# Cached attention with a token mixer on one core: the order of the last loads and of the last two pairs' steps

## Chip, cores and metric

The kernel runs on one NeuronCore of a Trainium2 chip. The metric is the device time of one execution in microseconds; lower is better.

## The reference

Two blocks work on the same normalised input and are added to it:

```python
xn = layernorm(x)                              # x: (8, 1, 512)
# A: grouped-query attention over a cache, one new token per sequence
q = (xn @ wq) in 32 heads of 128               # wq: (512, 4096)
k, v = caches of 8 heads x 8192 keys x 128     # per sequence, f32; 4 query heads share one
o = softmax(q k^T / sqrt(128)) v
A = o @ wo                                     # wo: (4096, 512)
# B: token mixer, an MLP over the token axis (one token), 1792 wide
B = gelu(layernorm(xn) * w1 + b1) . w2 + b2
out = x + A + B
```

All is f32. The caches of keys and values are 2 x 8 x 8 x 8192 x 128 x 4 bytes, some 537 of the 554 MB that the kernel loads; every byte of them is used once.

## The kernel before

The work is 64 pairs of a sequence and a key-value head (`N_IT`, numbered 0 to 63; `i = h * 8 + b`). Each pair has one load of keys and one of values, 4 MB each: a tile of 128 partitions x 64 rows x 128 numbers. The tiles lie in a ring of five buffers (`raw`, `RING = 5`), so a load takes the buffer of the load five places before it and can be issued when that one's readers are done.

**The loads.** `order` (lines 53 to 58) lists all loads with a sort key; `load_next` (L68) issues the next one on SyncE's DMA queue, each time some step frees a buffer: at the end of `qk(i)`, the scores of a pair (which frees its keys), and at the end of `pv(i)`, its values matmuls (which frees its values). The sort keys `2 i` for keys and `2 i + 2.5` for values make keys and values alternate, except for the last: `min(i, N_IT - 1.9)` gives keys 63 the key 124.2, and so the order at the end is keys 62, keys 63, values 61, values 62, values 63. Most loads are one DMA. Keys 0 come in four pieces of 16 rows, values 63 in pieces of 32, 16, 8 and 8 rows. When the list is empty, the next call loads the output weights of the last two heads into a ring buffer, in eight DMAs of 256 KB, four for each head (L82 to L86). The output weights of the other heads are loaded in the loop by `load_wo`.

**The steps of a pair.** `turn` (L215) transposes a quarter of the keys in 32x32 blocks, in place, on VectorE (L218). `qk` (L222) makes the scores on TensorE (L228), all four quarters being needed. `sm_max` takes the maximum of each partition on VectorE (L238); `sm_bias` spreads these over the partitions on TensorE (L243) and makes the correction from them on VectorE (L246); `sm_exp` makes the exponentials on ScalarE (L252); `sm_place` permutes them on TensorE (L259) and transposes them on VectorE (L261). `pv` (L267) multiplies them with the values on TensorE (L272); it can be called for a part of its 16 blocks of four rows. `o_pick` keeps the right blocks, three VectorE instructions (L283 to L287), and `o_place` puts them in place on TensorE (L294); for the last pair `o_last` does both in another way (L299, L300, L303). At a head's end come `o_sums` (L311, L313), `o_scale` (L316) and `o_project`, the product with the output weights (L326) that is added to `yacc` (L328).

**The order.** The kernel's instructions are issued on each engine in the order in which they are written (`manual_schedule`). `slot(i)` (L380) is one pair of the loop, for pairs 0 to 61, and interleaves the steps of pair i with the turns of pair i + 1 and the values matmuls of pair i - 1; the mixer's steps (`mx_begin`, `mx_step`, `mx_end`) are spread over the slots. The end, lines 418 to 445, is an order of its own, written out by hand, for the scores and softmax of pairs 62 and 63, the values matmuls of 61, 62 and 63, and the last projection.

Of the kernel before, what the change touches and what calls it, by code (L numbers as in the profile page):

```python
# [14 lines left out]
B, D, HQ, HKV, SK, DH, F = 8, 512, 32, 8, 8192, 128, 1792  # L15
REP = HQ // HKV
P = 128
NT = SK // P
# [9 lines left out]
N_IT = B * HKV  # L28
# [5 lines left out]
def attn_mixer_kernel(ctx: ExitStack, tc: tile.TileContext, x, kc, vc, wq, wo, w1, b1, w2, b2, out):  # L34
# [12 lines left out]
    def misc():  # L47
        return ps_m.tile([P, 512], F32, name="misc")
# [3 lines left out]
    KR, VR = {}, {}  # L52
    order = []
    for i in range(N_IT):
        order.append((2 * min(i, N_IT - 1.9), kc, KR, i))
        order.append((2 * i + 2.5, vc, VR, i))
    order.sort(key=lambda o: o[0])
    order.reverse()
# [9 lines left out]
    def load_next():  # L68
        if order:
            _, src, to, i = order.pop()  # L70
            h, b = divmod(i, B)
            t = ring.tile([P, NT, DH], F32, name="raw")
            rows = src[b, h].rearrange("(p t) d -> p t d", p=P)
            at = 0
            for n in (NT // 4,) * 4 if to is KR and i == 0 else (NT // 2, NT // 4, NT // 8, NT // 8) if not order else (NT,):
                nc.sync.dma_start(t[:, at:at + n, :], rows[:, at:at + n, :])
                at += n
            to[i] = t
        elif HKV - 1 not in wos:
            t = ring.tile([P, NT, DH], F32, name="raw")  # L80
            t = t.rearrange("p (h r c) d -> p h r (c d)", h=4, r=REP)
            for h in (HKV - 2, HKV - 1):  # L82
                rows = wo[h * REP * DH:(h + 1) * REP * DH, :].rearrange("(r p) n -> p r n", p=P)
                wos[h] = t[:, h % 2]
                for r in range(REP):
                    nc.sync.dma_start(wos[h][:, r, :], rows[:, r, :])  # L86

    wos = {}
# [15 lines left out]
    for _ in range(RING - 2):  # L104
        load_next()
# [109 lines left out]
    def turn(i, a, w=NT // 4):  # L215
        if i < N_IT:
            t = KR[i][:, a:a + w, :].rearrange("p t d -> p (t d)")
            nc.vector.transpose(t, t)  # L218
# [3 lines left out]
    def qk(i):  # L222
        h, b = divmod(i, B)
        S[i] = ps_s.tile([P, 512], F32, name="s")
        kt = KR.pop(i).rearrange("p (u g) d -> p g u d", g=NG)
        for j in range(NB):
            for g in range(NG):
                nc.tensor.matmul(S[i][g * Q:(g + 1) * Q, :], W[h % 2][:, b, j, :], kt[:, g, :, j * Q:(j + 1) * Q],  # L228
                                 start=(j == 0), stop=(j == NB - 1))
        load_next()  # L230
# [5 lines left out]
    def sm_max(i):  # L236
        mr = work.tile([P, 1], F32, name="mr")
        nc.vector.tensor_reduce(mr, S[i], AX.X, ALU.max)  # L238
        st[i] = mr

    def sm_bias(i):
        m = misc()
        nc.tensor.matmul(m[:, :P], st[i].to_broadcast([P, P]), ident, start=True, stop=True)  # L243
        t = one.tile([P, P], F32, name="sq")
        nb = work.tile([P, 1], F32, name="nb")
        nc.vector.tensor_tensor_reduce(t, m[:, :P], hmask, -SCALE, 3.0e38, ALU.add, ALU.min, nb)  # L246
        st[i] = nb

    def sm_exp(i):
        h, b = divmod(i, B)  # L250
        p = t2k.tile([P, 512], F32, name="t2k")
        nc.scalar.activation(p, S.pop(i), AF.Exp, bias=st[i], scale=SCALE, accum_out=LR[h % 2][:, b:b + 1])  # L252
        st[i] = p
# [3 lines left out]
    def sm_place(i):  # L257
        m = misc()
        nc.tensor.matmul(m, perm, st.pop(i), start=True, stop=True)  # L259
        PT[i] = work.tile([P, 512], F32, name="pt")  # L260
        nc.vector.transpose(PT[i], m)  # L261
# [5 lines left out]
    def pv(i, u0=0, u1=NU):  # L267
        if u0 == 0:
            O[i] = ps_o.tile([P, 512], F32, name="o")
        for u in range(u0, u1):  # L270
            c = u % NB
            nc.tensor.matmul(O[i][c * Q:(c + 1) * Q, :], PT[i][:, u * Q:(u + 1) * Q],  # L272
                             VR[i][:, u * NG:(u + 1) * NG, :].rearrange("p t d -> p (t d)"),
                             start=(u < NB), stop=(u >= NU - NB))
        if u1 == NU:
            del VR[i], PT[i]
            load_next()
# [3 lines left out]
    def o_pick(i):  # L281
        om = t2k.tile([P, 512], F32, name="t2k")
        nc.vector.tensor_tensor(om.rearrange("p (g d) -> p g d", g=NG), O.pop(i).rearrange("p (g d) -> p g d", g=NG),  # L283
                                dm.unsqueeze(2).to_broadcast([P, NG, DH]), ALU.mult)
        ob = work.tile([P, 256], F32, name="ob")
        nc.vector.tensor_add(ob, om[:, :256], om[:, 256:])  # L286
        nc.vector.tensor_add(ob[:, :DH], ob[:, :DH], ob[:, DH:])  # L287
        OB[i] = ob

    def o_place(i):  # L290
        h, b = divmod(i, B)
        if b == 0:
            MH[h] = ps_h.tile([P, 512], F32, name="mh")
        nc.tensor.matmul(MH[h][:, b * REP:(b + 1) * REP], OB.pop(i)[:, :DH], sel, start=True, stop=True)  # L294
# [13 lines left out]
    def o_sums(h):  # L308
        m = misc()
        for r in range(REP):  # L310
            nc.tensor.matmul(m[:, r * B:(r + 1) * B], sel[:, r:r + 1].to_broadcast([P, P]), LR[h % 2], start=True, stop=True)  # L311
        RD[h] = work.tile([P, REP, B], F32, name="rd")
        nc.vector.reciprocal(RD[h], m[:, :REP * B].rearrange("p (r b) -> p r b", r=REP))  # L313
# [60 lines left out]
    quart = NT // 4  # L374
# [3 lines left out]
    LAST = N_IT - 1  # L378
# [39 lines left out]
    h = HKV - 1  # L418
    qk(LAST - 1)
    turn(LAST, 0)  # L420
    sm_max(LAST - 1)
    turn(LAST, quart)
    sm_bias(LAST - 1)
    sm_exp(LAST - 1)
    turn(LAST, 2 * quart)
    sm_place(LAST - 1)
    turn(LAST, 3 * quart)
    qk(LAST)
    sm_max(LAST)
    sm_bias(LAST)  # L430
    sm_exp(LAST)
    pv(LAST - 2)
    o_pick(LAST - 2)
    o_place(LAST - 2)
    sm_place(LAST)
    pv(LAST - 1)
    o_pick(LAST - 1)
    o_place(LAST - 1)
    o_sums(h)
    for u0, u1 in ((0, 8), (8, 12), (12, 14), (14, 16)):  # L440
        pv(LAST, u0, u1)
    o_last(LAST)
    o_scale(h)
# [29 lines left out]
```

## Time and profile before

| | us |
|---|---|
| median of 3 runs | 1305.3 (1303.94 to 1306.02) |
| the profiled execution | 1303.8 |
| its span, first to last instruction | 1301.9 |
| busy in the span: TensorE matmuls, VectorE, ScalarE, GpSimd | 791.1, 805.8, 289.4, 231.0 |
| DMA, mean over the span | 426 GB/s, 554.5 MB |

The profile is one execution. PE is TensorE, PEld its weight loads, DVE VectorE, ACT ScalarE, POOL GpSimd, SP SyncE, which issues the DMAs; a q behind the name is the engine's sequencer, which issues and waits. A line such as L228 is a line of the kernel. A row of the timeline has the start and the length in microseconds, the engine, the line and operation, the tile written and those read, their shapes, the count of instructions merged in the row, and in brackets the idle time before it and what ended that. A row of the DMA issues has the count, the size of each and the time from issue to landing. The list of waits has the waiting engine and line, whom it waited for, the total, the count and the longest. A float32 matmul stands as two instructions in the counts: 16 matmuls of `pv` are 32.

### The profile page before, as it was taken

The page shows a single profiled execution, that of the slowest core. Times are in us where ns is not written, and L with a number is a line of the kernel's source. Part 1 is how long each engine was busy: PE and PEld are TensorE (multiplying, and loading weights), DVE is VectorE, ACT ScalarE, POOL GpSimd, SP SyncE. Part 2 cuts the span into 40 slices and gives each one's busy share as a digit, 9 for nine tenths or more (in the row PEclk, how much of TensorE's full clock was granted, in tenths as well). Part 3 has the DMA queues.
Part 4 walks back from the last instruction along what each step waited for, and adds up shares of the span by engine and source line. Part 5 has one row for each costly group of instructions (what it writes and reads, how often), then busy time and mean ns, then how long its engine had stood idle before and what let it go on. Part 6 is the DMA issues. An engine that isn't in the chain of part 4 may idle for free.

```text
span 1301.9 us, 12448 instructions
## 1 busy us (share of the span) xinstructions
PE 791.1 (61%) x5178; PEld 260.6 (20%) x5178; DVE 805.8 (62%) x834; ACT 289.4 (22%) x365; POOL 231.0 (18%) x244
## 2 busy tenths in 40 slices
PE   3375657755566646656558556575465775576466
PEld 2121112111121112211113111121112211122112
DVE  2676575575665665665765756755666657656662
ACT  0032221221222321212202213023121223213210
POOL 1022211212112211212112112022120222113210
PEclk9688777777778678687687786777776777767778
DMA  9999999999999999999999999999999999999995
GB/s 403 434 434 428 429 434 431 434 432 431 431 432 435 430 434 433 431 430 430 434 431 433 433 432 428 434 433 431 430 432 433 432 435 432 435 432 430 429 432 216
DMA packets 24139, 554.50 MB, mean 426 GB/s; under 512 B 2540, under 2 KB 2572, under 8 KB 6932
## 3 DMA queue, kind: packets, MB, share of 16 engines
q1 hardware_dynamic: 23940, 553.67, 98.9%
q8 instruction: 41, 0.67, 0.2%
q14 instruction: 14, 0.11, 0.0%
q0 software_dynamic: 128, 0.02, 0.0%
q10 hardware_dynamic: 16, 0.02, 0.0%
HBM read 553.69 MB, written 0.02 MB: 425 GB/s over the span
## 4 chain that ended last, share of the span: by engine, by line
DMA 58%; PE 22%; DVE 13%; issue 4%; ACT 3%; SPq 0%; ACTq 0%; DVEq 0%
DMA raw<-in_A_k_cache_dram 56%; DVE raw L218 10%; PE s L228 10%; PE o L272 6%; PE misc L259 3%; ACT L252 2%; DMA raw<-in_A_wq_dram 2%; DVE mr L238 1%; ACT t2k L252 1%; PE s L188 1%; PE misc L336 1%; PE misc L326 1%; PE misc L311 0%; DVE t2k L283 0%; DVE sq L246 0%
## 5 line engine op out<-in xcount | busy, mean ns | idle before, releaser
L218 DVE STREAM_TRANSPOSE raw<-raw 128x2048 f32<-128x2048 f32 x256 | 582.1, 2294 | 347.8 <-DMA raw<-in_A_k_cache_dram 347.8
L228 PE MATMUL s<-raw,w 128*32 128x512 f32 x2048 | 324.3, 790 | 20.3 <-issue 11.8
L347 POOL TENSOR_SCALAR g<-g,w2t 128x512 f32<-128x512 f32 x112 | 77.7, 693 | 897.5 <-ACT g L346 897.5
L272 PE MATMUL o<-raw,pt 128*32 128x512 f32 x2048 | 231.0, 592 | 0.0
L294 PE MATMUL mh<-sel,ob 128*128 128x4 f32 x126 | 35.0, 348 | 314.6 <-DVE ob L287 314.6
L252 ACT ACT_TABLE_LOAD x55 | 70.6, 1283 | 590.4 <-DVE nb L246 590.3
L348 POOL TENSOR_TENSOR macc<-macc,g 128x512 f32<-128x512 f32 x112 | 144.4, 1289 | 9.4
L259 PE MATMUL misc<-t2k,perm 128*128 128x512 f32 x128 | 125.0, 1077 | 17.2 <-ACT t2k L252 17.2
L228 PEld LDWEIGHTS s<-raw,w 128*32 128x32 f32 x2048 | 77.5, 144 | 279.5 <-issue 260.0
L346 ACT ACTIVATE g<-hb,b1t,w1t 128x512 f32<-128x512 f32 x112 | 91.0, 813 | 128.8 <-POOL macc L348 128.1
L243 PE MATMUL misc<-ident,mr 128*128 128x128 f32 x128 | 32.3, 336 | 127.7 <-DVE mr L238 127.7
L294 PEld LDWEIGHTS mh<-sel,ob 128*128 128x128 f32 x126 | 29.5, 290 | 328.6 <-DVE ob L287 328.6
L272 PEld LDWEIGHTS o<-raw,pt 128*32 128x32 f32 x2048 | 62.4, 110 | 156.9 <-issue 156.8
L252 ACT ACTIVATE t2k<-s,nb 128x512 f32<-128x512 f32 x64 | 44.0, 687 | 197.8 <-DVE nb L246 197.2
L261 DVE STREAM_TRANSPOSE pt<-misc 128x512 f32<-128x512 f32 x64 | 45.6, 712 | 39.1 <-PE misc L259 39.0
L346 ACT ACT_TABLE_LOAD x54 | 69.3, 1283 | 1.4
L238 DVE TENSOR_REDUCE mr<-s 128x1 f32<-128x512 f32 x64 | 42.2, 659 | 24.3 <-PE s L228 24.2
L243 PEld LDWEIGHTS misc<-ident,mr 128*128 128x128 f32 x128 | 19.6, 193 | 185.2 <-DVE mr L238 177.7
L283 DVE TENSOR_TENSOR t2k<-o,dm 128x512 f32<-128x512 f32 x63 | 43.2, 685 | 6.1 <-PE o L272 6.1
L211 DVE COPY w<-qt 32x128 f32<-32x128 f32 x64 | 37.0, 616 | 0.7
L259 PEld LDWEIGHTS misc<-t2k,perm 128*128 128x128 f32 x128 | 30.7, 297 | 21.6 <-ACT t2k L252 21.6
L286 DVE TENSOR_TENSOR ob<-t2k 128x256 f32<-128x256 f32 x63 | 26.8, 425 | 2.2
(75 smaller groups left out, 198.2 us busy)
## 6 DMA issues: line engine op xcount, KB each, us to landing
raw<-in_A_k_cache_dram SPq DMA_DIRECT2D x63, 4096.0 KB, 38.2
raw<-in_A_v_cache_dram SPq DMA_DIRECT2D x63, 4096.0 KB, 32.0
raw<-in_A_wq_dram SPq DMA_DIRECT2D x2, 4096.0 KB, 17.1
wo<-in_A_wo_dram SPq DMA_DIRECT2D x6, 1024.0 KB, 39.5
raw<-in_A_k_cache_dram SPq DMA_DIRECT2D x4, 1024.0 KB, 26.9
raw<-in_A_v_cache_dram SPq DMA_DIRECT2D x1, 2048.0 KB, 32.6
raw<-in_A_wo_dram SPq DMA_DIRECT2D x8, 256.0 KB, 7.3
raw<-in_A_v_cache_dram SPq DMA_DIRECT2D x1, 1024.0 KB, 34.7
```

The source lines that it names most:

```text
L218: nc.vector.transpose(t, t)
L228: nc.tensor.matmul(S[i][g * Q:(g + 1) * Q, :], W[h % 2][:, b, j, :], kt[:, g, :, j * Q:(j + 1) * Q], start=(j == 0), stop=(j == NB - 1))
L238: nc.vector.tensor_reduce(mr, S[i], AX.X, ALU.max)
L243: nc.tensor.matmul(m[:, :P], st[i].to_broadcast([P, P]), ident, start=True, stop=True)
L252: nc.scalar.activation(p, S.pop(i), AF.Exp, bias=st[i], scale=SCALE, accum_out=LR[h % 2][:, b:b + 1])
L259: nc.tensor.matmul(m, perm, st.pop(i), start=True, stop=True)
L261: nc.vector.transpose(PT[i], m)
L272: nc.tensor.matmul(O[i][c * Q:(c + 1) * Q, :], PT[i][:, u * Q:(u + 1) * Q], VR[i][:, u * NG:(u + 1) * NG, :].rearrange("p t d -> p (t d)") ...
L294: nc.tensor.matmul(MH[h][:, b * REP:(b + 1) * REP], OB.pop(i)[:, :DH], sel, start=True, stop=True)
L346: nc.scalar.activation(g, hb, AF.Gelu_apprx_tanh, bias=b1t[:, j:j + 1], scale=w1t[:, j:j + 1])
L347: nc.gpsimd.tensor_scalar(g, g, w2t[:, j:j + 1], 1.0, op0=ALU.mult, op1=ALU.mult)
L348: nc.gpsimd.tensor_add(acc, acc, g)
```

## The change

Three edits, all for the end of the kernel. The sort key of keys 63 is now 126, so that values 61 are loaded ahead of them, and keys 63 come in four pieces of 16 rows, one for each turn. The output weights of the last two heads are loaded in three DMAs: the last head but one in one of 1 MB, the last head in one of three quarters of that and one of a quarter. The steps of the last two pairs are put in a new order: the second turn of 63 ahead of the maximum of 62; the values matmuls of 61 ahead of the permuting of 62's exponentials (they were behind the softmax of 63); the picking of 61 behind the scores of 63; the values matmuls of 62 ahead of the permuting of 63's exponentials (they were behind it); the first eight blocks of the values matmuls of 63 ahead of the placing of 62 and the sums.

```diff
@@ the list of loads
-        order.append((2 * min(i, N_IT - 1.9), kc, KR, i))
+        order.append((2 * i, kc, KR, i))
@@ load_next
-            for n in (NT // 4,) * 4 if to is KR and i == 0 else (NT // 2, NT // 4, NT // 8, NT // 8) if not order else (NT,):
+            for n in (NT // 4,) * 4 if to is KR and i in (0, N_IT - 1) else (NT // 2, NT // 4, NT // 8, NT // 8) if not order else (NT,):
...
-                for r in range(REP):
+                for r in (slice(0, REP),) if h < HKV - 1 else (slice(0, REP - 1), slice(REP - 1, REP)):
                     nc.sync.dma_start(wos[h][:, r, :], rows[:, r, :])
@@ the end
     qk(LAST - 1)
     turn(LAST, 0)
+    turn(LAST, quart)
     sm_max(LAST - 1)
-    turn(LAST, quart)
     sm_bias(LAST - 1)
     sm_exp(LAST - 1)
     turn(LAST, 2 * quart)
+    turn(LAST, 3 * quart)
+    pv(LAST - 2)
     sm_place(LAST - 1)
-    turn(LAST, 3 * quart)
     qk(LAST)
+    o_pick(LAST - 2)
+    o_place(LAST - 2)
     sm_max(LAST)
     sm_bias(LAST)
     sm_exp(LAST)
-    pv(LAST - 2)
-    o_pick(LAST - 2)
-    o_place(LAST - 2)
+    pv(LAST - 1)
     sm_place(LAST)
-    pv(LAST - 1)
     o_pick(LAST - 1)
+    pv(LAST, 0, 8)
     o_place(LAST - 1)
     o_sums(h)
-    for u0, u1 in ((0, 8), (8, 12), (12, 14), (14, 16)):
+    for u0, u1 in ((8, 12), (12, 14), (14, 16)):
         pv(LAST, u0, u1)
     o_last(LAST)
     o_scale(h)
```

## The prediction

> **What bounds the kernel now.** I read the page first: the span, the bytes moved in each of 40 slices, and the chain that ended last.
>
> ```profile
> span 1301.9 us, 12448 instructions
> ...
> GB/s 403 434 434 428 429 434 431 434 432 431 431 432 435 430 434 433 431 430 430 434 431 433 433 432 428 434 433 431 430 432 433 432 435 432 435 432 430 429 432 216
> ...
> DMA 58%; PE 22%; DVE 13%; issue 4%; ACT 3%; SPq 0%; ACTq 0%; DVEq 0%
> ```
>
> For 39 of 40 slices the core moves bytes at one steady rate; only the last slice, 32.5 us long, falls to 216. So until then the kernel is bound by loading, and the edits, which all lie in the last two pairs, can only change what happens at the end. There I read the chain in order of time:
>
> ```profile
> 1207.40 38.54 DMA raw<-in_A_k_cache_dram
> ...
> 1258.39 3.84 PE s L228 x32
> ...
> 1271.30 6.02 PE s L228 x32
> ...
> 1296.87 1.93 PE misc L326 x64
> ...
> 1298.82 0.29 DVE yacc L328
> ```
>
> The last DMA on the chain is the load of keys 62 (pairs count from 0 to 63), landing at 1207.40 + 38.54 = 1245.94. Everything after it, 53.2 us to 1299.11, is compute. Then I read the issues of the DMA queue one by one (first fence: issue time and length) and how long each took to land (second fence, same order: values 62, the last piece of values 63, the last end weight).
>
> ```profile
> 1243.80 5.19 SPq L76 DMA_DIRECT2D raw<-in_A_v_cache_dram  x5
> ...
> 1248.55 0.43 SPq L76 DMA_DIRECT2D raw<-in_A_v_cache_dram  x1
> ...
> 1262.25 22.85 SPq L86 DMA_DIRECT2D raw<-in_A_wo_dram  x8
> ...
> 1284.77 0.33 SPq L86 DMA_DIRECT2D raw<-in_A_wo_dram  x1
> ```
>
> ```profile
> raw<-in_A_v_cache_dram SPq DMA_DIRECT2D x1, 4096.0 KB, 31.2
> ...
> raw<-in_A_v_cache_dram SPq DMA_DIRECT2D x1, 512.0 KB, 36.2
> ...
> raw<-in_A_wo_dram SPq DMA_DIRECT2D x1, 256.0 KB, 5.1
> ```
>
> Values 62 land at 1243.80 + 31.2 = 1275.0, values 63 at 1248.55 + 36.2 = 1284.75, the last end weight at 1284.77 + 5.1 = 1289.9. Three loads lie between 1245.94 and 1275.0, so one takes 9.7 us. The last byte is there 9.2 us before the end at 1299.11. That gap is what an order of the end can win; the loading itself it cannot shorten.
>
> **The change, part by part.** *Order of the loads.* Before, keys 63 land next after keys 62, then values 61. Now values 61 come first. By 9.7 us a load: values 61 at 1255.6, the four pieces of keys 63 at 1258.0, 1260.5, 1262.9 and 1265.3, values 62 at 1275.0, values 63 as before. Each takes the ring buffer that its place in the order now gives it (values 61 after the score matmuls of pair 60, keys 63 after the values matmuls of pair 59), which are the same two moments exchanged, 20 us and more before the data are due: no dry spell of the queue, cost nothing.
>
> *Smaller pieces.* Nearest row: values 63 come in four pieces already and land 9.75 us after values 62, against 9.7 for a whole load. I take 0.1 us for keys 63, paid by all that lands behind: values 62 at 1275.1, values 63 at 1284.85. The other bound is in the rivals.
>
> *End weights in three loads.* An issue on this queue waits for the landing of an earlier one:
>
> ```profile
> SPq L86 <- DMA raw<-in_A_v_cache_dram: 20.0, 6, 9.3
> ```
>
> Six of the eight end-weight issues waited so, the last until 1284.77. The rows fit a rule of eight: each issue waits until the one eight before it has landed (the last end weight goes out 0.02 us after the last piece of values 63, which is eight before it). Count with the new order: third and fourth piece of values 63 wait for values 61 (1255.6) and the first piece of keys 63 (1258.0), the three end weights for the other pieces (1260.5 to 1265.3, their buffer being free at 1262.2). All are queued 20 us before they are served. Does that bring the last landing forward? The two stretches around 1284.75 (columns: busy us by engine, clock, DMA share, GB/s):
>
> ```profile
> 1280.00:1284.75 4.75, 3.08 (x26) 0.91 (x16) 1.41 (x3) 0.00 (x0) 0.00 (x0) 1.00 0.78 292
> 1284.75:1289.90 5.15, 3.99 (x33) 0.94 (x32) 1.77 (x3) 0.00 (x0) 0.00 (x0) 1.00 0.64 242
> ```
>
> Some of the 16 engines ran out of work. But 2 MB of weights landed in the 5.15 us behind the last values, 0.64 us for each 256 KB or 410 GB/s: the slowest engine, which sets a landing, was hardly idle. So I leave the last landing where it is plus 0.1, at 1290.0. The other bound: the 292 x 4.75 + 242 x 5.15 = 2,630 KB at the 431 GB/s of the slices take 6.1 us from 1280, landing at 1286.1.
>
> *The steps' order.* Rows of before, VectorE, then TensorE, then ScalarE:
>
> ```profile
> 1258.67 2.30 DVE L218 STREAM_TRANSPOSE raw<-raw 128x2048 f32<-128x2048 f32 x1
> ...
> 1268.97 2.27 DVE L218 STREAM_TRANSPOSE raw<-raw 128x2048 f32<-128x2048 f32 x1
> 1277.35 0.69 DVE L238 TENSOR_REDUCE mr<-s 128x1 f32<-128x512 f32 x1 [6.10 <-PE s L228]
> 1278.73 0.29 DVE L246 CUSTOM_DVE_ANT_0 sq<-misc,hmask 128x128 f32<-128x128 f32 x1 [0.69 <-PE misc L243]
> ...
> 1285.21 0.72 DVE L261 STREAM_TRANSPOSE pt<-misc 128x512 f32<-128x512 f32 x1 [1.44 <-PE misc L259]
> ```
>
> ```profile
> 1266.23 2.07 PE L259 MATMUL misc<-t2k,perm 128*128 128x512 f32 x2 [2.73 <-ACT t2k L252]
> ...
> 1278.10 0.49 PE L243 MATMUL misc<-ident,mr 128*128 128x128 f32 x2 [0.82 <-DVE mr L238]
> 1278.51 3.64 PE L272 MATMUL o<-raw,pt 128*32 128x512 f32 x32
> ...
> 1284.07 1.10 PE L259 MATMUL misc<-t2k,perm 128*128 128x512 f32 x2
> ...
> 1290.34 0.39 PE L294 MATMUL mh<-sel,ob 128*128 128x4 f32 x2 [1.60 <-DVE ob L287]
> ...
> 1291.56 3.64 PE L272 MATMUL o<-raw,pt 128*32 128x512 f32 x32
> 1295.81 1.05 PE L303 MATMUL mh<-selg,t2k 128*128 128x4 f32 x8 [0.62 <-DVE t2k L299]
> ```
>
> ```profile
> 1279.06 0.69 ACT L252 ACTIVATE t2k<-s,nb 128x512 f32<-128x512 f32 x1 [12.89 <-DVE nb L246]
> ```
>
> From 1258.67 on I lay the new order out. VectorE: first turn 1258.67 (its piece landed at 1258.0), second turn to 1263.2 (landed 1260.5). Only then the maximum of pair 62, 0.9 us later than its scores allow (1258.39 + 3.84 = 1262.2); behind the second turn wait the whole softmax of 62 and so ScalarE and TensorE. Maximum to the correction's end is 1.67 us (1277.35 to 1279.02), so 1264.9; exponentials to 1265.7; turns three and four 1264.9 to 1269.4 (landed 1262.9, 1265.3). TensorE: L243 at 1263.9, values matmuls of 61 at 1264.3 to 1267.9 (their rows: 0.41 after L243, 3.6 long), permuting matmul of 62 to 1269.0, in the shadow of the turns. Scores of 63 start at 1269.4, 1.9 us before today's 1271.30, and, with TensorE busy just before, take 3.84 and not 6.02: end 1273.3 against 1277.32. That is 4.0 of the gain. The picking of pair 61 (1.6 us, the idle time ahead of L294) lies beside these scores on VectorE, nothing waits for it.
> Softmax of 63: L243 of it at 1274.05; the values matmuls of 62 stand next on TensorE and wait for values 62 at 1275.1, to 1278.75; permuting to 1279.85, transposition to 1280.6. First half of the values matmuls of 63 (1.8) to 1282.45, while VectorE picks 62 (to 1282.2). Placing and sums 1.22 (1290.34 to 1291.56): 1283.7. The second half: 0.9 to 1284.6, 0.45, then the last piece, landed 1284.85, to 1285.5. From the end of these matmuls to that of L303 it is 1.63 today (1295.23 to 1296.86): 1287.15. The projection takes 1.93; with all weights there, 1289.1. They are not: the first head's half of the rows runs at once, the last MB lands in two loads at 1289.4 and 1290.0, whose 24 and 8 matmuls (0.03 each) end at 1290.4. With 0.03 and 0.29 for yacc: 1290.7 against 1299.11.
>
> **Sum:** 8.4 us less, of which 9.2 is the old wait behind the last byte, less 0.7 of new and 0.1 of later landing. The profiled execution took 1303.8 us (span 1301.9 and 1.9 around it), so 1295.4 on its footing; it lies 1.5 below the median 1305.3, and 1305.3 - 8.4 = 1296.9 is the forecast. What is late next is the last end weight, with compute 1.3 us behind that (1290.7 - 1289.4); so most errors of up to a microsecond in the steps cost nothing.
>
> **The rivals.** *Cold clock.* TensorE's granted clock (next-to-last number but one) fell in the end of before:
>
> ```profile
> 1245.33:1248.74 3.41, 1.83 (x20) 0.30 (x12) 2.70 (x2) 0.00 (x0) 0.00 (x0) 1.00 1.01 428
> 1248.74:1252.15 3.41, 0.49 (x2) 0.30 (x2) 3.41 (x3) 0.00 (x0) 0.00 (x0) 1.00 1.05 452
> ...
> 1262.39:1265.81 3.42, 0.49 (x2) 0.30 (x2) 3.42 (x5) 0.41 (x1) 0.00 (x0) 1.00 0.95 412
> 1265.81:1269.22 3.41, 2.07 (x2) 0.50 (x2) 2.66 (x3) 0.36 (x2) 0.00 (x0) 0.50 0.98 423
> ```
>
> A stretch with 0.49 us of matmuls was followed by half clock, one with 1.83 by full clock. In the new order the gap of 1262.2 to 1264.3 has 0.49 in it and matmuls after it: at least 1.7 us in any such stretch, just above or at what kept the clock. If it falls, the values matmuls of 61 take 6.02/3.84 as long (+2.1), the permuting one 2.07 instead of 1.10, at worst the scores 63 +2.2: up to 5.3 on a compute path with 1.3 + 0.7 us of slack in front of it, up to 3.3 at the end: 1297 to 1300.2, about 1298.5. The Trainium skill, "TensorE: Matmul & The Clock Gate", part 1, lets the clock fall after an idle window of about 3.4 us; by that this rival could not happen. The trace differs: it fell with 2.73 us as the longest idle time (row of L259), so the rival stays.
> *Pieces cost a fixed time.* The first keys are in four pieces today:
>
> ```profile
> 1.65 0.64 SPq L76 DMA_DIRECT2D raw<-in_A_k_cache_dram  x1
> ...
> 3.49 0.50 SPq L76 DMA_DIRECT2D raw<-in_A_k_cache_dram  x1
> ```
>
> ```profile
> raw<-in_A_k_cache_dram SPq DMA_DIRECT2D x1, 1024.0 KB, 23.6
> ...
> raw<-in_A_k_cache_dram SPq DMA_DIRECT2D x1, 1024.0 KB, 30.4
> ```
>
> The first landed at 25.25, the fourth at 33.9: 8.6 for three MB, not 7.3. Those 1.3 us, 1.2 over what I took, would move every later landing and the end: 1298.1. Against it: values 63 paid 0.1. The Trainium skill, "DMA: Bandwidth & Descriptors", section "Anatomy of one DMA", fits a fixed 2.0 us to a DMA (issued from GpSimd); three more in series would by my estimate add 6 us. No row here shows that for queued loads.
> *Pieces are waited for as one.* If a turn or a values matmul is released only by its whole tile, cutting brings nothing: the first turn starts at 1265.4, the second ends at 1270.0, the maximum of 62 slips 6.8 us, TensorE is cold by then (values matmuls of 61 from 1271.1, some 5.5 long by the clock of before, 4.75 us to full clock in its scores 63), scores 63 end at 1281.8, values matmuls of 62 at 1286.7; through 1.1, 0.75, 1.8, 1.22, 1.8, 1.63, 1.93 and 0.32 the end is 1297.3 to 1297.8, gain 1.5: 1303.8, no change by measure. Against it: the pieces of values 63 were issued within 5.19 us for five loads, unheld by each other though they write one tile.
> *The queue runs dry* (slower). SP issues in order, and a held issue holds all behind it. Should my rule of eight be wrong so that late pieces are issued only as the one just before them lands, each such wait empties the queue for about 4.5 us (the lone weight's 5.1 less 0.64 of transfer). Two waits eat the 8.4; three, say the last two pieces of values 63 and the weights, end 5.1 later than before: 1310.4. For it: the six waits above happened on this queue. Against: the count of eight.
>
> **How the numbers follow.** Forecast 0.70; cold clock 0.10, fixed time 0.09 (both still faster); waited for as one 0.07 (same); dry queue 0.04 (slower). About 0.2%, 2.6 us, is what a measurement of this kernel can tell from no change; so faster 0.89, same 0.07, slower 0.04. Range: below, the early landing of 1286.1, with which compute ends at 1289.4 (gain 9.7, 1295.6) less 1.1 for the spread of the runs (1303.94 to 1306.02); above, the cold clock's 1300.2. So 1294.5 to 1300.2.
>
> **What would show it.** Right: the chain's last DMA is no longer keys 62 but an end weight or late values; yacc ends within 1.5 us of the last weight's landing; the scores 63 take about 3.9 and start near 1269.4; the first turn of 63 starts before the fourth piece lands; no end-weight issue waits past 1266. Wrong: a first turn at 1265 or later (tile waited for whole), 0.50 as granted clock around 1266 to 1272 (cold), the last landing after 1291.5 (fixed time) or a hole in the GB/s before 1280 (dry queue). A gain under 5 us would make the forecast wrong.

## The result, and the profile after

| | before, us | after, us |
|---|---|---|
| median | 1305.25 (4 runs, 1303.94 to 1306.02) | 1296.17 (4 runs, 1295.80 to 1296.71) |
| ratio of the two | | 0.9932, 95% interval 0.9915 to 0.9949 |
| profiled execution | 1303.8 | 1296.24 |
| its span | 1301.9 | 1294.3 |

Faster by 9.1 us by the medians (by the interval 6.7 to 11.1), by 7.6 between the two profiled executions; 1296.9 was forecast. The page of the changed kernel, the same lines as before:

```profile
span 1294.3 us, 12448 instructions
...
GB/s 405 434 426 430 427 436 435 429 430 436 430 429 436 431 431 433 433 431 431 432 432 434 433 428 433 435 430 432 434 429 432 436 431 428 436 434 432 429 431 322
...
DMA 60%; PE 21%; DVE 12%; issue 4%; ACT 3%; SPq 0%; ACTq 0%; DVEq 0%
```

Thirty-nine slices are as they were, within 8 GB/s each. The last one moved 322 GB/s instead of 216: the kernel moves the same bytes in all, and the program now ends sooner behind the last of them. The chain that ended last, in order of time:

```profile
1208.21 38.12 DMA raw<-in_A_k_cache_dram
...
1258.79 4.29 PE s L228 x32
...
1263.52 26.30 DMA raw<-in_A_wo_dram
1289.81 0.14 issue
1289.95 1.11 PE misc L326 x32
...
1291.08 0.29 DVE yacc L328
```

Where before 53 us of compute stood behind keys 62 without another transfer, the chain now ends in the landing of an end weight at 1289.81 and the 16 matmuls (32 instructions) of the last head. The scores of 62 stand ahead of that load because they free its buffer; its 26.30 us are long because other loads were issued before it (x5's last weight, issued when the last values had landed, takes 5.13). Keys 62 landed at 1246.33, 0.4 later than in the profile of before, ahead of any edit; so read the other times against that. Issues of the queue and, in the same order, their sizes and times to landing (first piece of keys 63, last piece of values 63, the three end weights):

```profile
1228.13 0.33 SPq L76 DMA_DIRECT2D raw<-in_A_k_cache_dram  x1
...
1258.46 0.33 SPq L76 DMA_DIRECT2D raw<-in_A_v_cache_dram  x1
1263.09 0.38 SPq L86 DMA_DIRECT2D raw<-in_A_wo_dram  x1
1263.52 10.29 SPq L86 DMA_DIRECT2D raw<-in_A_wo_dram  x1
1273.85 7.26 SPq L86 DMA_DIRECT2D raw<-in_A_wo_dram  x1
```

```profile
raw<-in_A_k_cache_dram SPq DMA_DIRECT2D x1, 1024.0 KB, 30.3
...
raw<-in_A_v_cache_dram SPq DMA_DIRECT2D x1, 512.0 KB, 26.8
raw<-in_A_wo_dram SPq DMA_DIRECT2D x1, 1024.0 KB, 24.7
raw<-in_A_wo_dram SPq DMA_DIRECT2D x1, 768.0 KB, 26.3
raw<-in_A_wo_dram SPq DMA_DIRECT2D x1, 256.0 KB, 16.6
```

The first piece of keys 63 landed at 1258.4, the last of values 63 at 1285.3, the last weight at 1290.45; the last two are 38.9 and 44.1 us behind keys 62, where before it was 38.8 and 43.9. The loads became neither faster nor, to speak of, slower. The last piece of values 63 went out at 1258.46, when the first piece of keys 63, eight issues before it, had just landed (1258.4): the prediction's rule of eight. Now VectorE, then TensorE (start, length, instruction, in brackets the idle time before it and what ended that):

```profile
1259.06 4.49 DVE L218 STREAM_TRANSPOSE raw<-raw 128x2048 f32<-128x2048 f32 x2
1263.48 0.65 DVE L238 TENSOR_REDUCE mr<-s 128x1 f32<-128x512 f32 x1
...
1265.03 4.50 DVE L218 STREAM_TRANSPOSE raw<-raw 128x2048 f32<-128x2048 f32 x2
...
1273.30 0.69 DVE L238 TENSOR_REDUCE mr<-s 128x1 f32<-128x512 f32 x1 [1.80 <-PE s L228]
```

```profile
1264.60 3.64 PE L272 MATMUL o<-raw,pt 128*32 128x512 f32 x32
1268.17 1.12 PE L259 MATMUL misc<-t2k,perm 128*128 128x512 f32 x2
1269.59 3.64 PE L228 MATMUL s<-raw,w 128*32 128x512 f32 x32 [0.29 <-DVE raw L218]
...
1275.66 3.64 PE L272 MATMUL o<-raw,pt 128*32 128x512 f32 x32 [1.13 <-DMA raw<-in_A_v_cache_dram]
```

The first turn starts at 1259.06, before the second, third and fourth piece have landed (the second came at 1260.9, when the issue that waited for it went on). The scores of 63 start at 1269.59 (before: 1271.30) and take 3.64 instead of 5.97. The values matmuls of 62 wait 1.13 us for their values: from here on compute runs at the pace of the loads. And the clock (the third number from the end) stayed up over the whole end:

```profile
1260.27:1294.30 34.03, 25.35 (x248) 9.67 (x240) 14.76 (x22) 1.93 (x5) 0.00 (x0) 1.00 0.79 330
```

### The profile page after: what moved, and what is told of

It is laid out like the page before. It is cut to its first block, busy times and chain, and to the rows that moved or that the text cites. A ratio compares the mean times of both kernels' runs of the same rounds, so it can differ in the third digit from the quotient of the medians.

```text
span 1294.3 us, 12448 instructions
## 1 busy us (share of the span) xinstructions
PE 783.8 (61%) x5178; PEld 260.0 (20%) x5178; DVE 805.3 (62%) x834; ACT 289.4 (22%) x365; POOL 231.2 (18%) x244
## 4 chain that ended last, share of the span: by engine, by line
DMA 60%; PE 21%; DVE 12%; issue 4%; ACT 3%; SPq 0%; ACTq 0%; DVEq 0%
DMA raw<-in_A_k_cache_dram 57%; DVE raw L218 10%; PE s L228 9%; PE o L272 5%; PE misc L259 3%; DMA raw<-in_A_wo_dram 2%; ACT L252 2%; DMA raw<-in_A_wq_dram 2%; DVE mr L238 1%; ACT t2k L252 1%; PE s L188 1%; PE misc L336 1%; PE misc L326 1%; PE misc L311 0%; DVE t2k L283 0%
## 5 line engine op out<-in xcount | busy, mean ns | idle before, releaser
L228 PE MATMUL s<-raw,w 128*32 128x512 f32 x2048 | 315.3, 770 | 16.9 <-issue 11.8
L294 PE MATMUL mh<-sel,ob 128*128 128x4 f32 x126 | 35.0, 348 | 311.4 <-DVE ob L287 311.4
L294 PEld LDWEIGHTS mh<-sel,ob 128*128 128x128 f32 x126 | 29.5, 291 | 325.4 <-DVE ob L287 324.5
```

## The experiments

The theory: the order of the steps makes the gain, the new order and sizes of the loads only keep up with it, and the end is now the last weight's landing with compute close behind. The main rival: the loads make the gain, through fewer held issues and the swap.

| kernel | median, us | ratio to before, 95% interval |
|---|---|---|
| before, in the sets of x1 to x4 and of x5 to x7 | 1304.72, 1304.87 | |
| changed (before in its set: 1305.25) | 1296.17 | 0.9932 (0.9915 to 0.9949) |
| x1 new steps, old loads | 1295.53 | 0.9931 (0.9916 to 0.9945) |
| x2 old steps, new loads | 1305.07 | 1.0002 (0.9992 to 1.0011) |
| x3 keys 63 ahead of values 61 again | 1296.06 | 0.9935 (0.9920 to 0.9950) |
| x4 keys 63 whole | 1301.96 | 0.9979 (0.9969 to 0.9989) |
| x5 eight end weights | 1296.14 | 0.9934 (0.9921 to 0.9946) |
| x6 no end weights loaded | 1294.93 | 0.9927 (0.9915 to 0.9940) |
| x7 values matmuls of 61 late | 1301.33 | 0.9974 (0.9965 to 0.9983) |

**x1, the steps alone.** The loads' lines are those of before, lines 418 on those of the changed kernel.

```diff
-        order.append((2 * i, kc, KR, i))
+        order.append((2 * min(i, N_IT - 1.9), kc, KR, i))
...
-            for n in (NT // 4,) * 4 if to is KR and i in (0, N_IT - 1) else ...
+            for n in (NT // 4,) * 4 if to is KR and i == 0 else ...
...
-                for r in (slice(0, REP),) if h < HKV - 1 else (slice(0, REP - 1), slice(REP - 1, REP)):
+                for r in range(REP):
```

> The loads of before (keys 63 whole and ahead of values 61, eight end weights) with the new order of the last two pairs' steps. My theory: the steps bring nearly all of the gain, and the last end weight's landing, about 44 us behind that of keys 62, stays where it is. Values 61 land about 1265.7, so the values matmuls of 61 start there and not at 1264.6; if TensorE keeps full clock the end is within 0.3 us of the changed kernel's 1291.4, if it falls to half clock up to 1.7 us later: 1296 to 1298.5 us. Rival (the new order and size of the loads bring the gain): within 2.5 us of before, 1303 to 1306.

1295.53 us, the whole gain; it lies 0.5 below the lower end of what was expected. TensorE, and the end of the chain:

```profile
1265.52 3.64 PE L272 MATMUL o<-raw,pt 128*32 128x512 f32 x32 [1.09 <-DMA raw<-in_A_v_cache_dram]
...
1270.15 3.64 PE L228 MATMUL s<-raw,w 128*32 128x512 f32 x32
```

```profile
1284.87 5.18 DMA raw<-in_A_wo_dram
1290.06 0.04 issue
1290.10 0.47 PE misc L326 x8
...
1290.59 0.29 DVE yacc L328
```

The values matmuls of 61 do wait for their values, 1.09 us, and the scores of 63 start 0.6 later than in the changed kernel; that is taken up where the changed kernel waits 1.13 us for values 62. The clock held (3.64 for each). With the small last weights only 8 instructions stand behind the last landing in the chain, not 32.

**x2, the loads alone.** The changed kernel with lines 418 on as before.

> The new loads (values 61 first, keys 63 in four pieces, three end weights) with the old order of steps. My theory: compute from the landing of keys 62 on is the chain as before, 53 us, so no change: 1304.5 to 1306; the last weight lands about 44 us behind keys 62 and is then waited for by nobody. Rival: 1297 to 1300.

1305.07, no change. The third end weight, and the end of the chain:

```profile
raw<-in_A_wo_dram SPq DMA_DIRECT2D x1, 256.0 KB, 16.6
```

```profile
1291.63 5.31 PE o L272 x32
...
1300.52 0.29 DVE yacc L328
```

The weight, issued at 1273.52, is there at 1290.1, 8.4 us before the projection starts at 1298.5. The rival falls. (In this one execution the last values matmuls ran at half clock, 5.31 and not 3.61; the last section comes back to it.)

**x3, the swap undone.**

```diff
-        order.append((2 * i, kc, KR, i))
+        order.append((2 * min(i, N_IT - 1.9), kc, KR, i))
```

> The changed kernel with keys 63 (in four pieces) ahead of values 61 again. My theory: the swap alone is worth little. Values 61 land about 1265.7, 1.1 us after the values matmuls of 61 could start; with full clock that is taken up by the wait for values 62 at 1275.6, and the end is the same: 1296.2 within 0.5. If the idle time drops TensorE to half clock, up to 1.7 us more: 1298. Rival (the swap is what lets the new steps run): 4 us or more, 1300 and up.

1296.06, the same as with the swap. The row of the values matmuls of 61:

```profile
1265.56 3.64 PE L272 MATMUL o<-raw,pt 128*32 128x512 f32 x32 [0.98 <-DMA raw<-in_A_v_cache_dram]
```

Again a wait of one microsecond that the later wait for values 62 takes in.

**x4, keys 63 whole, the swap kept.**

```diff
-            for n in (NT // 4,) * 4 if to is KR and i in (0, N_IT - 1) else ...
+            for n in (NT // 4,) * 4 if to is KR and i == 0 else ...
```

> The changed kernel with keys 63 in one load. My theory: the two turns now ahead of the maximum of 62 wait for the whole load at about 1265.7 instead of starting at 1259.1, the maximum of 62 starts at 1270.3 instead of 1263.5, TensorE is cold, and the end is 5.9 us later: 1302.1, between 1300.5 and 1303.5. Rival (the pieces are waited for as one tile, or the turns have room enough): no more than 1 us, 1296 to 1297.2.

1301.96, 5.8 above the changed kernel. VectorE, TensorE and the end:

```profile
1265.12 4.50 DVE L218 STREAM_TRANSPOSE raw<-raw 128x2048 f32<-128x2048 f32 x2 [6.52 <-DMA raw<-in_A_k_cache_dram]
1269.55 0.65 DVE L238 TENSOR_REDUCE mr<-s 128x1 f32<-128x512 f32 x1
```

```profile
1270.98 5.54 PE L272 MATMUL o<-raw,pt 128*32 128x512 f32 x32
```

```profile
1296.49 0.29 DVE yacc L328
```

VectorE idles 6.52 us, until the whole load has landed, and the maximum of 62, whose scores are long done, waits in its queue behind two turns of the next pair. TensorE goes to half clock meanwhile (5.54 for 3.64). So with the swap the pieces are needed, and it is shown that a turn is released by its own piece.

**x5, eight end weights.**

```diff
-                for r in (slice(0, REP),) if h < HKV - 1 else (slice(0, REP - 1), slice(REP - 1, REP)):
+                for r in range(REP):
```

> The changed kernel with the last two heads' weights in eight loads again. My theory: the last five go out only as earlier loads land, the last one at about 1285.3, and land 0.64 us apart, the last at 1290.4 as in the changed kernel: no change, 1296.2 within 0.5. Rival (the waits of these issues held up the end): 2 us or more, 1298 and up.

1296.14, no change. The end of the chain:

```profile
1285.16 5.13 DMA raw<-in_A_wo_dram
1290.30 0.04 issue
1290.34 0.47 PE misc L326 x8
```

The last weight goes out only at 1285.16, held until the last values landed, and still lands where it did, at 1290.3. So the last landing does not follow the time at which its issue goes out: in the changed kernel that was 1273.85.

**x6, the end weights not loaded.** 2 MB less; their place is taken by weights that are there.

```diff
-        elif HKV - 1 not in wos:
-            t = ring.tile([P, NT, DH], F32, name="raw")
...
-                    nc.sync.dma_start(wos[h][:, r, :], rows[:, r, :])
...
+    wos[h - 1] = wos[h] = wos[h - 2]
     qk(LAST - 1)
```

> The changed kernel without the load of the last two heads' weights; the last projection uses the weights of the head before them, so 2 MB are not loaded. My theory: the end of the changed kernel is the last weight's landing with compute about 1.1 us behind it, so the end moves to where compute is by itself: L303 ends at about 1288, the projection at 1289.9, yacc at 1290.2, and the time falls by 1.1 us, to 1295.1, between 1294.4 and 1295.7. Rival (loading bounds the end through and through): the end follows the last byte, 5.2 us sooner, 1291. Other rival (compute alone bounds it): no change, 1296.2.

1294.93, 1.2 below the changed kernel; the lines of this kernel are 8 less than elsewhere (L318 is L326).

```profile
1243.33 31.90 DMA raw<-in_A_v_cache_dram
...
1287.57 1.93 PE misc L318 x64
...
1289.52 0.29 DVE yacc L320
```

yacc ends at 1289.81, 43.9 us behind keys 62 (1245.9 here), against 45.0 in the changed kernel: compute was 1.1 us behind the weights, as worked out. Neither rival holds: with 5 us of loading gone, 1.2 are won. The last transfer of this chain is values 62, landing at 1275.23; behind it stand 14.6 us of compute without another wait in the chain.

**x7, the values matmuls of 61 late again.**

```diff
-    pv(LAST - 2)
     sm_place(LAST - 1)
     qk(LAST)
-    o_pick(LAST - 2)
-    o_place(LAST - 2)
     sm_max(LAST)
     sm_bias(LAST)
     sm_exp(LAST)
+    pv(LAST - 2)
+    o_pick(LAST - 2)
+    o_place(LAST - 2)
     pv(LAST - 1)
```

> The changed kernel with the values matmuls of 61, their picking and placing behind the softmax of 63 again, the rest as changed. My theory: TensorE has nothing between the correction of 62 and the scores of 63 but the permuting, is at half clock for the scores (6.0 us, end about 1275.5 and not 1273.2), and then has two values matmuls, with the picking of 61 between them, in the chain where it had one: the end is 5.2 us later, 1301.4, between 1299 and 1303. Rival (the end is set by the last load anyway): no more than 1 us, 1296 to 1297.2.

1301.33, 5.2 above the changed kernel. TensorE:

```profile
1270.23 6.47 PE L228 MATMUL s<-raw,w 128*32 128x512 f32 x32 [2.48 <-DVE raw L218]
...
1277.94 3.64 PE L272 MATMUL o<-raw,pt 128*32 128x512 f32 x32
1283.25 0.39 PE L294 MATMUL mh<-sel,ob 128*128 128x4 f32 x2 [1.67 <-DVE ob L287]
1283.57 3.64 PE L272 MATMUL o<-raw,pt 128*32 128x512 f32 x32
```

Both prices are there: without work ahead of them the scores run at half clock (6.47 against 3.64), and two values matmuls with a picking between them stand in the chain, so those of 62 start at 1283.57 and not 1275.66. The profiled execution, 1302.92, is the slowest of the ten, 1.6 above their median, so these rows show which prices are paid and not how large each is in the median; whether the clock fell in all ten is not shown. By the medians this move of three steps is worth over half of the gain. The other moves were not tried one by one.

## Why the prediction was right

*The bound and the gap.* That the last byte was there 9.2 us before the end, and that the order of the steps can win this and no more, held: the loads of x2 change nothing, the steps of x1 everything. From the landing of keys 62 to the end of yacc it was 53.2 us before and is 45.0 now: 8.1 won, where the sum says 8.4. *The loads' order at no cost* held, and x3 shows what the prediction left unsaid, that it brings nothing either: the swap needs the pieces (x4, 5.8 us), and without the swap the pieces are not needed (x1). *Pieces at 0.1 us* held: values 63 landed 38.9 us behind keys 62, against 38.8. *End weights: last landing unmoved* held: 44.1 against 43.9, and the same with eight loads (x5). One sign did not come out as forecast: no end-weight issue was to go out past 1266, and the third went out at 1273.85, behind the 10.29 us of the second. That was no wait for a landing, and it moved no landing. *The steps* came to within some 0.3 us of the worked-out times up to the scores of 63 (1269.4 worked out, 1269.59 measured) and within 0.6 at the values matmuls of 62 (1275.1 and 1275.66), 0.4 of it the later keys 62. *What is late next*: the last weights, with compute 1.3 behind; 1.1 measured (x6).

Two terms were a little off. The projection's end behind the second weight load: 0.96 was reckoned from its landing, 0.14 + 1.11 measured. The 32 instructions ran without a gap, and the 32 ahead of them took as long, so the 0.03 for each was a little small; the third load, there at 1290.45, held nothing up. And the sum, 8.4 us, was made against an execution that lies 1.5 below the median and then taken off the median; by the medians it is 9.1, by the profiled pair 7.6. Both lie inside the interval. In x2, with the old steps, keys 62 to yacc took 54.8 and not 53.2, for its last values matmuls ran at half clock; so the old end itself can differ between executions, and the sum has no term for that.

Of the rivals, the one on pieces waited for as one tile is answered by the first turn at 1259.06 and by x4, whose 1301.96 shows about what it would have cost. The cold clock did not come in the changed kernel, x1 or x3; in the changed kernel the two stretches of 3.4 us from 1260.27 on hold 2.75 and 2.92 us of matmuls, where the prediction reckoned with at least 1.7. x4 and x7 show it where TensorE was left without work. In x7 the stretch from 1265.74 to 1269.16 holds 1.13 us of matmuls and was followed by half clock, so 0.49 is not where the limit lies. The Trainium skill, "TensorE: Matmul & The Clock Gate", part 1, wants an idle window of about 3.4 us for the clock to fall. Here too the trace differs: in x7, from 1262.33 (granted clock 1.00) to the scores of 63, no idle time of TensorE is over 2.48 us. A fixed time for each piece and a dry queue did not show.

## What to carry to other kernels

When a kernel is bound by loading until its last transfers, measure the time from the last landing to the end; that gap, not any busy share, is what an order of the last steps can win, and laying the rows of the old trace into the new order gave it to within a microsecond. Move work that is ready into the idle time ahead of a step that waits: it takes itself out of the tail and keeps TensorE's clock up for the step behind it (x7: 5.2 us for one move). Test the parts of such a change alone: here the two edits of the loads were needless (x1), and the swap alone, without the pieces, would have cost most of the gain (x4).

## What the runs showed of the hardware

Two things were not expected. First, the second and third end-weight issues of the changed kernel occupied SyncE for 10.29 and 7.26 us (rows above), where each of the eight small ones takes 0.33:

```profile
L86 SPq DMA_DIRECT2D raw<-in_A_wo_dram x8: 327/328/431, 1262.3 to 1284.8; - x8
```

(This row is of before: lengths in ns, least, median and most.) No semaphore wait stands in these 10.29 us; they came while several loads were queued ahead, and x2 and x3 have such long issues as well. Only the third end weight stood behind the second, and x5, in which the last weight goes out later still, ends at the same time, so they cost nothing here; what holds such an issue was not tried.

Second, the clock does not follow the matmul time of a stretch alone. In x2, the two stretches around the start of the last values matmuls:

```profile
1289.15:1292.56 3.41, 2.21 (x22) 1.59 (x26) 1.43 (x4) 0.00 (x0) 0.00 (x0) 1.00 0.06 22
1292.56:1295.97 3.41, 3.41 (x24) 0.89 (x18) 0.00 (x0) 0.00 (x0) 0.00 (x0) 0.50 0.00 0
```

2.21 us of matmuls were followed by half clock, where 1.83 had kept it up in the profile of before. Of the 2.21, about 1.3 were matmuls of 4 and 8 columns (L294 and L311); that these count for little is a guess. It cost that execution 1.7 us in the last values matmuls, and it is a likely reason, not a shown one, that the runs with the old steps spread over some 2 us (1303.94 to 1306.02) and those of the changed kernel over 0.9.
